# The key weights' path in four chunks, with a new order of every step, in a fused attention and FFN kernel

## The chip, the cores and the metric

The kernel runs on one core of a Trainium2 chip. The metric is the device time of one execution in microseconds (us); three executions before the change gave 151.39 us as their median (150.9 to 152.2).

The core has five instruction streams that run side by side and meet only at semaphores: TensorE (PE in the profile; its weight loads are listed as PEld), VectorE (DVE), ScalarE (ACT), GpSimd (POOL) and SyncE (SP), which here only issues DMAs. ScalarE can issue DMAs as well. Each stream executes in program order.

## The reference, cut to what matters

```python
xn = layernorm(x)                                     # x: 2048 x 448
q, k, v = heads(xn @ wqkv)                            # 16 heads of 28
pq, pk = q @ w_phi, k @ w_phi                         # 28 x 28 per head
phi(p) = concat(softmax(p), softmax(-p))              # 56 features per head
kv = phi(pk).T @ v;   z = sum over tokens of phi(pk)
o = (phi(pq) @ kv) / (phi(pq) . z + 1e-6)
h = xn @ w1 + b1
out = x + o @ wo + (h * tanh(softplus(h))) @ w2       # "mish", 1792 wide
```

## The kernel before, in words

**Tiles.** The 2048 tokens are 16 tiles of 128, handled as 8 pairs u = 0..7 (tiles 2u and 2u+1). The width 448 is three chunks of 128 rows and a tail of 64; the tail of two tiles shares one 128-row chunk, and so most matmuls work on half rows (64 of 128), two tiles side by side.

**Folded weights.** The feature map is folded into the weights: Wpk = Wk x blockdiag(w_phi) and Wpq = Wq x blockdiag(w_phi). For that Wk is loaded (`load_main`, line 272, three chunks, and `load_tail`, line 279, the last 64 rows twice), turned on TensorE (`w_tr`, line 550), brought to SBUF as WT, and multiplied with the block-diagonal Wbd (`w_mm`, line 573) into PSUM, from where the result goes to the tile Wpk. WT lies in the buffer Eq0, and so the profile shows its evacuations as writes of Eq. Wq is turned on the way by four DMA transposes (`load_qT`, line 284) and multiplied likewise into Wpq. In the kernel before, `w_tr` and `w_mm` work on halves h = 0, 1 of two chunks each: the first half's two turned chunks lie in two PSUM banks and are evacuated by ScalarE and VectorE side by side ("both"), the second half's by one instruction of one engine.

**Stages.** For each pair: statistics of the layer norm (`ln_stats`, VectorE, or three instructions of ScalarE), the reciprocal root (`ln_rstd`, ScalarE or GpSimd), the normalised pair xn (`ln_pair`, VectorE or GpSimd), its transpose xnT (`xT`, line 518, by TensorE with an evacuation, or by a DMA on SP). Then, on TensorE, V, K and Q of the pair (`v_mm`, `k_mm`, `q_mm`, all through `pair_part`, whose matmuls have line 438), each in a part 1 of 8 matmuls and a part 2 of 6. ScalarE takes exp(+) and exp(-) of K (line 623) and of Q (line 684), 4 pairs' V go through ScalarE (line 514) and 4 through VectorE (line 516). K's exponentials are normalised (`k_norm`: sum and reciprocal on VectorE, product on GpSimd), and all pairs are gathered into one KV matrix (`kv_mm`, line 652), which `kvz` masks and turns by a DMA into KVZ. Q's exponentials lie in one of three slots (`Eq_of`: slot 0 in the tile Eq, slots 1 and 2 in rows of actT) and are turned by one DMA per tile (`q_turn`, line 692, into EqT); pair u uses slot u mod 3, so that the exponentials of a later pair wait until the transposes of the earlier pair in the same slot have landed.

The FFN's first layer (`ffn1`) is 28 blocks of 14 matmuls (line 438 again, 512 columns) with one Mish on ScalarE each (line 703). Then come attention's second product (`nd`, line 726, with seven VectorE instructions), the transpose of o (`oT`, line 761), and the output sums of the FFN and of wo in common PSUM banks (`pair_out`, line 866; the last tiles in `ffn2` and `wo`, lines 828 and 844), which VectorE adds to x (line 793), and SP stores.

**PSUM.** There are 8 banks; most blocks take a pair (`take2`, line 391), the least recently used, and hold it until the evacuation.

**What sets the order.** Nothing is scheduled at run time: the table `ORDER` (line 147) names some 310 steps, `run_order` calls them in turn, and each appends its instructions to its engines' streams. Semaphore waits are worked out from the order (`Program.resolve`). In a name, the digits are the pair, tile or block, and a last letter is the engine (s: SP, a: ScalarE, d: VectorE, p: GpSimd, m: DMA): `lkms` loads the main part of Wk from SP, `wtk0b` turns half 0 of Wk and evacuates it on both engines. z12 is 12 matmuls on constants at the start.

Of the kernel before, what the change touches and what calls it, by code (L numbers as in the profile page):

```python
# [160 lines left out]
"""


# [5 lines left out]
def _kernel(es, nc, A_x, A_wqkv, A_w_phi, A_wo, B_w1, B_b1, B_w2, out):  # L169
# [62 lines left out]
    def Eq_of(u):  # L232
        if u % 3 == 0:
# [2 lines left out]

    oT_home = [(Wkv, 0, ["Wk", "Wv"]), (Wkv, 14 * P, []), (WqT, 0, ["Wq"]), (Wp[1], 0, ["Wp1"])]
    home_rows = {"Wk": [("Wk", 0), ("Wt", 0), ("Wt", 1)], "Wv": [("Wv", 0)], "Wq": [("WqT", g) for g in range(G)] + [("WqTd",)],
                 "Wp1": [("Wp", 1, h, c) for h in range(2) for c in range(2)]}

    homes_taken = set()

# [10 lines left out]
    def bank16(b):  # L253
        return PS.bitcast(BF16)[:, 2 * b * TCW:2 * (b + 1) * TCW]
# [7 lines left out]
    def pb(b):  # L262
        return ("ps", b)
# [140 lines left out]
    def take1():  # L404
        b = min((b for b in range(8) if b - b % 2 not in held), key=lambda b: used[b])
        touch(b)
        return b
# [139 lines left out]
                ap_on(mask[:, 2 * r:2 * r + 1], [[0, G], [1, 2], [0, DH]]), ALU.mult),  # L547
               r=[("Wraw",), ("mask",), ("Wbd0",)], w=[("Wbd", r)], tag=f"Wbd{r}")

    def w_tr(h, eng):  # L550
        b = take2(False) if eng == "both" else take1()

        def oT(c):
            if eng == "both":
                return bank16(b + c)[0:GP, 0:G * P].rearrange("p (g n) -> p g n", g=G)
            return bank16(b)[0:GP, c * G * P:(c + 1) * G * P].rearrange("p (g n) -> p g n", g=G)

        def tr(e):
            for c in range(2):
                for g in range(G):  # L560
                    ins = e.transpose(oT(c)[:, g, :], Wk[:, 2 * h + c, g * GP:(g + 1) * GP], ident[:])  # L561
            return ins
        r = rows_of("Wk")[:1 + 2 * h] + [("ident",)]
        if eng == "both":
            pe(tr, r, [pb(b), pb(b + 1)], f"wtr1{h}")
            for c, (en, res) in enumerate((("ACT", "WT"), ("DVE", "WU"))):
                evac(en, lambda c=c: WT[h][:, c], lambda c=c: oT(c), [pb(b + c)], [(res, h)], f"wtre1{h}.{c}")
            return
        pe(tr, r, [pb(b)], f"wtr1{h}")
        evac(eng, lambda: WT[h].rearrange("p c g n -> p (c g n)"), lambda: bank16(b)[0:GP, 0:2 * G * P], [pb(b)],  # L570
             [("WT", h), ("WU", h)], f"wtre1{h}")

    def w_mm(which, h, eng):
        b = take2(False)
        n = GP

        def lhs(c, g):
            if which:
                return WT[h][:, c, g, :]
            return WqT[0:GP, g, (2 * h + c) * P:(2 * h + c + 1) * P]  # L580

        def mm(e):
            for c in range(2):
                for g in range(G):
                    ins = e.matmul(bank(b + c)[:, g * n:(g + 1) * n], lhs(c, g), Wbd[:, g, :, 0:n // 2],  # L585
                                   start=True, stop=True)
            return ins
        pe(mm, ([("WT", h), ("WU", h)] if which else [("WqT", g) for g in range(G)] + [("WqTd",)]) + [("Wbd", 0), ("Wbd", 1)], [pb(b), pb(b + 1)], f"wmm{which}{h}")
        if which and eng == "both":
            for c, en in enumerate(("ACT", "DVE")):  # L590
                evac(en, lambda c=c: Wp[1][:, 2 * h + c, :], lambda c=c: bank(b + c)[:, 0:D], [pb(b + c)],
                     [("Wp", 1, h, c)], f"wmme1{h}.{c}")
            return
        if which:
            evac(eng, lambda: Wp[1][:, 2 * h:2 * h + 2, :], lambda: two(b, D), [pb(b), pb(b + 1)], [("Wp", 1, h, 0), ("Wp", 1, h, 1)],
                 f"wmme1{h}")
            return

        for c in range(2):
            evac(eng, lambda c=c: Wp[0][:, 2 * h + c, :].rearrange("p (g r n) -> p r g n", r=2, n=QP),  # L600
                 lambda c=c: bank(b + c)[:, 0:D].rearrange("p (r g n) -> p r g n", r=2, n=QP), [pb(b + c)],
                 [("Wp", 0, 2 * h + c)], f"wmme0{h}.{c}")

# [314 lines left out]
    for t in range(NT):  # L918
# [92 lines left out]
```

## Time and profile before

| what | value |
|---|---|
| median of the three runs | 151.39 us (150.9 to 152.2) |
| the profiled execution | 151.12 us |
| its span, first to last instruction | 149.2 us (1.92 us lie around it) |
| granted TensorE clock | 1.0 |
| busy: DVE, ACT, POOL | 101.7, 73.5, 41.7 us |
| DMA traffic | 17.24 MB, mean 116 GB/s; 271 to 303 GB/s in the slices from 3.7 to 14.9 us |

The profile is one execution. Its first part gives the busy time of each engine; the chain is followed back from the last instruction to what released it; the waits name the instruction that a waiting engine waited for; the timeline lists instructions by start, and an x behind a row merges neighbours of one form. Matmul ends are modelled and overlap the next start by up to 0.17 us, so starts are the better measure of TensorE's pace. For DMAs the landing is counted from the start of the issue.

### The profile page before, as it was taken

Reading aid. Unit: us, or ns where it says so; the run is one execution under the profiler, and the core shown is the slowest. Engines: PE = TensorE matmul, PEld = TensorE weight load, DVE = VectorE, ACT = ScalarE, POOL = GpSimd, SP = SyncE. Lnnn points to the kernel's source line nnn. Section 1 sums busy time; section 2 is a strip of 40 time slices with the busy share of each in tenths; the row PEclk is TensorE's granted clock in tenths of the full one; section 3 lists DMA queues with packets and bytes.
Section 4 is the critical chain, followed back from the end, with each engine's and each line's share of the span. In section 5 each row is a group of like instructions: output and inputs, shape, how many; then the busy total and the mean of one; then the engine's idle time right before and its main releaser. Section 6 shows DMA issues by size and latency. Waiting matters only on the chain.

```text
span 149.2 us, 3996 instructions
## 1 busy us (share of the span) xinstructions
PE 143.6 (96%) x1731; PEld 74.0 (50%) x1731; DVE 101.7 (68%) x226; ACT 73.5 (49%) x91; POOL 41.7 (28%) x60
## 2 busy tenths in 40 slices
PE   7799999999969999999999999999999999999993
PEld 2375555555424494444444455555555555455442
DVE  0999999999999303196675919999979495303342
ACT  3799999999679599766567580202000000000000
POOL 7607476999989930000000000000000000000000
DMA  5998988999939507999703030214100400700333
GB/s 132 282 303 271 202 136 117 177 241 203 178 72 196 88 4 146 245 320 195 157 4 62 4 62 0 42 24 40 28 4 0 123 4 19 166 4 0 125 121 123
DMA packets 39997, 17.24 MB, mean 116 GB/s; under 512 B 33964, under 2 KB 39212, under 8 KB 39980
## 3 DMA queue, kind: packets, MB, share of 16 engines
q1 hardware_dynamic: 39228, 16.64, 51.1%
q10 hardware_dynamic: 752, 0.35, 1.2%
q8 instruction: 13, 0.21, 0.6%
q14 instruction: 4, 0.03, 0.1%
HBM read 7.02 MB, written 1.84 MB: 59 GB/s over the span
## 4 chain that ended last, share of the span: by engine, by line
PE 86%; DMA 6%; ACT 3%; SPq 2%; DVE 1%; issue 0%; ACTq 0%
PE PS L438 44%; PE PS L866 31%; PE PS L828 3%; DMA Wkv<-in_A_wqkv_dram 3%; PE PS L726 2%; DMA EqT<-actT 2%; PE PS L652 2%; SPq L692 2%; PE PS L585 1%; ACT actT L684 1%; ACT actT L623 1%; PE PS L844 1%; PE PS L561 1%; ACT v_all L514 1%; SPq L270 1%; PE PS L509 1%
## 5 line engine op out<-in xcount | busy, mean ns | idle before, releaser
L438 PE MATMUL PS<-xnT,W 64*128 64x512 bf16 x392 | 45.1, 376 | 1.3 <-ACT actT L684 1.3
L703 ACT ACTIVATE actT<-PS,b1T 128x1024 bf16<-128x1024 f32 x28 | 29.8, 1112 | 20.9 <-PE PS L438 19.7
L866 PE MATMUL PS<-W,actT 64*128 64x448 bf16 x392 | 38.7, 349 | 0.0
L438 PEld LDWEIGHTS PS<-xnT,W 64*128 64x128 bf16 x392 | 18.1, 94 | 22.5 <-ACT actT L684 1.8
L866 PEld LDWEIGHTS PS<-W,actT 64*128 64x128 bf16 x392 | 18.4, 94 | 17.7
L635 POOL TENSOR_TENSOR actT<-actT,rSk 128x896 bf16<-128x896 bf16 x16 | 26.6, 1699 | 0.7 <-DVE rSk L633 0.7
L793 DVE TENSOR_TENSOR x_all<-PS,x_all 128x448 bf16<-128x448 f32 (+1 forms) x16 | 9.2, 615 | 16.1 <-PE PS L866 15.2
L631 DVE TENSOR_REDUCE Sk<-actT 128x32 f32<-128x896 bf16 x16 | 16.7, 1043 | 0.0
L741 DVE COPY Sq<-PS 128x16 f32<-128x16 f32 x32 | 4.0, 167 | 15.8 <-PE PS L726 15.8
L623 ACT ACTIVATE actT<-PS 128x896 bf16<-128x896 f32 x16 | 13.7, 923 | 0.9 <-PE PS L438 0.8
L438 PE MATMUL PS<-Wkv,xnT 64*128 64x448 bf16 x112 | 12.7, 349 | 0.0
L438 PE MATMUL PS<-Wpk,xnT 64*128 64x448 bf16 x112 | 12.6, 349 | 0.0
L438 PE MATMUL PS<-Wpq,xnT 64*128 64x448 bf16 x112 | 12.4, 349 | 0.0
L467 DVE BATCH_NORM_STATS2 stats<-x_all 128x6 f32<-128x448 bf16 x14 | 8.4, 604 | 3.7 <-DMA x_all<-in_A_x_dram 3.7
L749 DVE TENSOR_TENSOR v_all<-v_all 128x464 f32<-128x464 f32 x16 | 10.3, 642 | 0.6
L745 DVE TENSOR_TENSOR v_all<-PS,Sq 128x464 f32<-128x464 f32 x16 | 10.3, 641 | 0.5
L752 DVE TENSOR_TENSOR xn<-v_all,rden 128x448 bf16<-128x448 f32 x16 | 10.0, 625 | 0.6
L747 DVE TENSOR_TENSOR v_all<-PS,Sq 128x464 f32<-128x464 f32 x16 | 10.1, 630 | 0.0
L684 ACT ACTIVATE actT<-PS 128x896 bf16<-128x896 f32 x10 | 8.6, 920 | 2.2 <-DMA EqT<-actT 1.9
L438 PEld LDWEIGHTS PS<-Wpq,xnT 64*128 64x128 bf16 x112 | 5.5, 94 | 5.2
L438 PEld LDWEIGHTS PS<-Wkv,xnT 64*128 64x128 bf16 x112 | 5.4, 94 | 5.1
L438 PEld LDWEIGHTS PS<-Wpk,xnT 64*128 64x128 bf16 x112 | 5.4, 94 | 5.0
(89 smaller groups left out, 128.1 us busy)
## 6 DMA issues: line engine op xcount, KB each, us to landing
W<-in_B_w_dram SPq DMA_DIRECT2D x1, 1568.0 KB, 9.0
out_dram<-x_all SPq DMA_DIRECT2D x7, 224.0 KB, 2.3
W<-in_B_w_dram SPq DMA_DIRECT2D x3, 448.0 KB, 4.9
x_all<-in_A_x_dram SPq DMA_DIRECT2D x2, 448.0 KB, 4.7
x_all<-in_A_x_dram SPq DMA_DIRECT2D x3, 224.0 KB, 3.2
Wkv<-in_A_wqkv_dram SPq DMA_DIRECT2D x2, 336.0 KB, 4.7
Wo<-in_A_wo_dram SPq DMA_DIRECT2D x2, 336.0 KB, 3.8
W<-in_B_w_dram SPq DMA_DIRECT2D x2, 224.0 KB, 3.6
```

Of the source, the lines that this page charges most:

```text
L438: ins = e.matmul(o, lhs(c, k), rhs(c, k), start=part == "1" and c == 0, stop=part == "2" and c == 2)
L623: op("ACT", lambda e, s=s: e.activation(E_of(u)[:, s, :, :], two(b, D), ACT.Exp, scale=1.0 if s == 0 else -1.0), r=[pb(b), pb(b + 1)], w=[ ...
L631: op("DVE", lambda e: e.tensor_reduce(Sk[u][:, s, :], Eh(), AX.X, ALU.add), r=[("E", u, s)], w=[("Sk", u, s)], tag=f"Sk{u}.{s}")
L635: op("POOL", lambda e: e.tensor_tensor(Eh(), Eh(), ap_on(rSk[u][:, s, 0:1], [[1, 2 * H], [0, DH]]), ALU.mult), r=[("E", u, s), ("rSk", u, ...
L684: op("ACT", lambda e, s=s: e.activation(Eq_of(u)[:, :, s, :].rearrange("p i (h n) -> p i h n", n=64)[:, :, :, 0:QP], two(b, D).rearrange(" ...
L703: op("ACT", lambda e: e.activation(actT[:, fc, q * 1024:(q + 1) * 1024], bank(b, 2), ACT.Mish, bias=b1T[:, fc:fc + 1]), r=[("b1T",), pb(b) ...
L745: op("DVE", lambda e: e.tensor_tensor(tv(t1[i]), num(0), sx(1), ALU.mult), r=[pb(b), pb(b + 1), ("Sq", i, 1)], w=[("t1", i)], tag=f"ta{t}")
L747: op("DVE", lambda e: e.tensor_tensor(tv(t2), num(1), sx(0), ALU.mult), r=[pb(b), pb(b + 1), ("Sq", i, 0)], w=[("t2",)], tag=f"tb{t}")
L749: op("DVE", lambda e: e.tensor_tensor(t1[i], t1[i], t2, ALU.add), r=[("t1", i), ("t2",)], w=[("t1", i)], tag=f"tc{t}")
L752: op("DVE", lambda e: e.tensor_tensor(o_sb[(t // 2) % 2][:, t % 2, :].rearrange("p (h d) -> p h d", d=DH), t1[i][:, :, 0:DH], ap_on(rden[i ...
L793: op("DVE", lambda e: e.tensor_tensor(x_all[:, t, 0:n], bank(b)[:, 0:n], x_all[:, t, 0:n], ALU.add), r=[pb(b), ("x", t)], w=[("out", t)], ...
L866: ins = e.matmul(bank(places[par][0])[:, 0:D], l, r, start=fresh[par], stop=places[par][2] and i >= len(todo) - 2)
```

## The change

- Wk's path works on one chunk c = 0..3 at a time: one PSUM bank, four transposes and one evacuation for each `w_tr`, four matmuls and one evacuation for each `w_mm`. Chunk 3 alone waits for the loads of the tail. Wq's `w_mm` is split in four likewise, and only its chunk 3 waits for the doubled tail columns.
- Evacuations of the K side: the turned chunks 2 and 1 by ScalarE, 0 and 3 by VectorE; all four of Wpk, and all four of Wpq, by ScalarE.
- Wk's main part is SP's second load. x of pair 1, the bias and the main part of Wv are issued by ScalarE, behind its table load.
- The statistics that two of the tiles (7 and 15) had on ScalarE are on VectorE. Pairs 2, 4 and 5 are normalised by GpSimd (before: 7 and 0). Pair 1's transpose is evacuated by VectorE alone.
- The table is a new one. Of VectorE's work in the first 20 us it makes: statistics of tiles 6 and 7, normalisation of pair 3, then tiles 3, 2, 5, 4, normalisation of pair 1, its transpose's evacuation, tiles 14, 15, 12, 9, 8, 10, normalisation of pair 7, tile 11, V of pair 1. The load of tiles 12 to 15 stands on SP behind Wq's four transposes, where it stood ahead of them. Wo and W2 are loaded before KVZ is made, where it was after.

The diff, without most of the table:

```diff
 ORDER = """
-pm pw lx3s pp1 pp2 pp0 pk lx1s lkms lkts st6d lpa table pi st7a st2d st3d rs3t xn3d lvms rs1a xn1d lbs z12 lx2s lx0a
...
+lpa pp2 lx3s pm z12 st6d pi lkms table st7d pw lx1a lkts lba lvma bd rs3t wtk2a xn3d lx2s lqT2 wtk0d st3d pv wtk1a wmk2a
+xt3a wtk3d lqT1 wmk0a wmk1a st2d wmk3a st5d v31d rs1p lqT0 st4d xn1d rs2p lqT3 b1 qd lx6s v32a k31 lx0s wmq1a lx4s pp1
...
-    def w_tr(h, eng):
-        b = take2(False) if eng == "both" else take1()
...
+    def w_tr(c, eng):
+        b = take1()
+        to = bank16(b)[0:GP, 0:G * P].rearrange("p (g n) -> p g n", g=G)
 
         def tr(e):
-            for c in range(2):
-                for g in range(G):
-                    ins = e.transpose(oT(c)[:, g, :], Wk[:, 2 * h + c, g * GP:(g + 1) * GP], ident[:])
+            for g in range(G):
+                ins = e.transpose(to[:, g, :], Wk[:, c, g * GP:(g + 1) * GP], ident[:])
             return ins
...
+        pe(tr, rows_of("Wk")[:1 if c < 3 else 3] + [("ident",)], [pb(b)], f"wtr{c}")
+        evac(eng, lambda: WT[c // 2][:, c % 2], lambda: to, [pb(b)], [("WT", c)], f"wtre{c}")
...
+    def w_mm(which, c, eng):
+        b = take1()
+
+        def lhs(g):
+            if which:
+                return WT[c // 2][:, c % 2, g, :]
+            return WqT[0:GP, g, c * P:(c + 1) * P]
+
+        def mm(e):
+            for g in range(G):
+                ins = e.matmul(bank(b)[:, g * GP:(g + 1) * GP], lhs(g), Wbd[:, g, :, 0:GP // 2], start=True, stop=True)
+            return ins
+        r = [("WT", c)] if which else [("WqT", g) for g in range(G)] + ([("WqTd",)] if c == 3 else [])
+        pe(mm, r + [("Wbd", 0), ("Wbd", 1)], [pb(b)], f"wmm{which}{c}")
+        if which:
+            evac(eng, lambda: Wp[1][:, c, :], lambda: bank(b)[:, 0:D], [pb(b)], [("Wp", 1, c)], f"wmme1{c}")
             return
```

What the new table moves, at three places.

The first is the start of SP's queue, the loads. Before:

```order
L270 DMA x_all<-in_A_x_dram 128x896 x2
L273 DMA Wkv<-in_A_wqkv_dram 128x3x448
L281 DMA Wkv<-in_A_wqkv_dram 64x896 x2
L273 DMA Wkv<-in_A_wqkv_dram 128x3x448
L302 DMA b_rows<-in_B_b_dram 14x128
L270 DMA x_all<-in_A_x_dram 128x896
L270 DMA x_all<-in_A_x_dram 128x1792
L285 DMA_TRANSPOSE WqT<-in_A_wqkv_dram 128x448 x4
```

The change (the first L273 is Wk in both; the second, before, is Wv; the load of 1792 columns holds tiles 12 to 15):

```order
L270 DMA x_all<-in_A_x_dram 128x896
L273 DMA Wkv<-in_A_wqkv_dram 128x3x448
L281 DMA Wkv<-in_A_wqkv_dram 64x896 x2
L270 DMA x_all<-in_A_x_dram 128x896
L285 DMA_TRANSPOSE WqT<-in_A_wqkv_dram 128x448 x4
L270 DMA x_all<-in_A_x_dram 128x1792
```

One x load and Wv have left the queue ahead of Wq's transposes, and the load of tiles 12 to 15 has moved behind them.

The second is TensorE's first real work. Before:

```order
L376 MATMUL PS<-const-bfloat16-1.0 128x512 x12
L561 MATMUL PS<-ident,Wkv 112x128 x8
L509 MATMUL PS<-ident,xn 128x128 x7
L561 MATMUL PS<-ident,Wkv 112x128 x8
L509 MATMUL PS<-ident,xn 128x128 x7
L697 MATMUL PS<-ident,b_rows 128x14
L585 MATMUL PS<-Wbd,Eq 128x112 x16
L438 MATMUL PS<-Wkv,xnT 128x448 x22
```

The change (L556 is the turning of Wk, L571 the product, L509 the transpose of a pair, L674 that of the bias):

```order
L376 MATMUL PS<-const-bfloat16-1.0 128x512 x12
L556 MATMUL PS<-ident,Wkv 112x128 x12
L571 MATMUL PS<-Wbd,Eq 128x112 x4
L509 MATMUL PS<-ident,xn 128x128 x7
L556 MATMUL PS<-ident,Wkv 112x128 x4
L571 MATMUL PS<-Wbd,Eq 128x112 x12
L438 MATMUL PS<-Wkv,xnT 128x448 x8
L674 MATMUL PS<-ident,b_rows 128x14
L438 MATMUL PS<-Wkv,xnT 128x448 x6
L438 MATMUL PS<-Wpk,xnT 128x448 x8
L571 MATMUL PS<-Wbd,WqT 128x112 x8
L509 MATMUL PS<-ident,xn 128x128 x7
```

The products of Wk come between the turnings; V of pair 3 starts with one pair's transpose behind it where it was two, and the other pair's stands between the products of Wq.

The third is the middle of SP's queue, where the turning of Q's exponentials (EqT) meets the last chunks of W1 (L277). Before, from the last two transposes of xn on:

```order
L521 DMA_TRANSPOSE xnT<-xn 128x7x128 x2
L277 DMA W<-in_B_w_dram 128x1792 x2
L692 DMA_TRANSPOSE EqT<-Eq 128x8x128 x2
L692 DMA_TRANSPOSE EqT<-actT 128x8x128 x3
L692 DMA_TRANSPOSE EqT<-Eq 128x8x128
```

The change:

```order
L521 DMA_TRANSPOSE xnT<-xn 128x7x128 x2
L669 DMA_TRANSPOSE EqT<-actT 128x8x128
L277 DMA W<-in_B_w_dram 128x1792
L669 DMA_TRANSPOSE EqT<-actT 128x8x128
L669 DMA_TRANSPOSE EqT<-Eq 128x8x128
L669 DMA_TRANSPOSE EqT<-actT 128x8x128
L669 DMA_TRANSPOSE EqT<-Eq 128x8x128
L669 DMA_TRANSPOSE EqT<-actT 128x8x128
L669 DMA_TRANSPOSE EqT<-Eq 128x8x128
L669 DMA_TRANSPOSE EqT<-actT 128x8x128 x2
L312 DMA Wo<-in_A_wo_dram 128x3x448 x2
L312 DMA Wo<-in_A_wo_dram 64x448 x2
```

One chunk of W1 stands there where two stood (the other is loaded earlier), and a transpose of slot 2 (tile 5) has moved ahead of it. The tiles are 7, 6, 9, 5, 4, 13 before, and 5, then 4, 6, 8, 7, 9, 12, 10, 11 in the change; behind Wo follow tile 13 and W2.

More of the change, by code (lines that the diff above doesn't have):

```diff
@@ new lines @@
+wmq0a xn2p l1ts xt1d st14d st15d wmq2a wmq3a k32 k11 st12d rs7p st9d q11 xt2m st8d k12 st10d xn7d q31 rs4p v11d pp0 q12
+xn4p st11d v12d q21 rs5p st13d q32 q22 xn5p k21 st0d l1m2s l1m0s rs6p xt7m v21d k22 st1d v22a ep e3 rs0p v71a pk xt4m
+k71 v72a kn3.1 xn6d k72 xt5m k41 xn0d kn3.0 e2 xt6m xt0m v41d e5 k42 l1m1s v42d e4 q41 v51d q42 e6 e8 v52a kn2.0 k61
+v61d k62 kn4.0 k01 k51 kn7.0 kn4.1 k02 v62d q51 k52 q52 kn0.0 e7 q61 e9 v01d q62 e12 kn1.1 kn6.1 e10 f0.11 e11 kn1.0
+v02d f0.12 kn0.1 f1.01 f0.21 f1.02 f1.21 kn7.1 f1.31 f1.22 los kn2.1 q71 f1.32 f1.51 kn5.0 f0.22 e13 f1.52 q01 q72 q02
@@ L161 @@
+wo7F sto2 G42 wo7H sto0 wo42 g15 stt14 sto3 sto4 stt15
 """
@@ L238, in _kernel @@
     home_rows = {"Wk": [("Wk", 0), ("Wt", 0), ("Wt", 1)], "Wv": [("Wv", 0)], "Wq": [("WqT", g) for g in range(G)] + [("WqTd",)],
-                 "Wp1": [("Wp", 1, h, c) for h in range(2) for c in range(2)]}
+                 "Wp1": [("Wp", 1, c) for c in range(4)]}
     homes_taken = set()
@@ L346, in p_pads @@
             op("POOL", lambda e, i=i: e.memset(Eq_of(i).rearrange("p i s (h n) -> p (i s h) n", n=64)[:, :, QP:64], 0.0),
-               w=[("Eqp", i)] + ([(n, h) for n in ("WT", "WU") for h in range(2)] if i == 0 else []), tag=f"pp{i}")
+               w=[("Eqp", i)] + ([("WT", c) for c in range(4)] if i == 0 else []), tag=f"pp{i}")
     def p_mask2():
@@ L558, in tr @@
         def tr(e):
-            for c in range(2):
-                for g in range(G):
-                    ins = e.transpose(oT(c)[:, g, :], Wk[:, 2 * h + c, g * GP:(g + 1) * GP], ident[:])
-            return ins
[L563 to L567, printed above, removed]
-            return
@@ L569, in w_tr @@
[L569 to L602, printed above, removed]
@@ L625, in then @@
                    r=[pb(b), pb(b + 1)], w=[("E", u, s)], tag=f"exk{u}.{s}")
-        pair_part(f"k{u}", part, tok_works(u, Wp[1]), [("xnT", u), ("xnU", u)] + [("Wp", 1, h, c) for h in range(2) for c in range(2)], then)
+        pair_part(f"k{u}", part, tok_works(u, Wp[1]), [("xnT", u), ("xnU", u)] + [("Wp", 1, c) for c in range(4)], then)
     def k_norm(u, s):
@@ L922, in _kernel @@
         add(f"stt{t}", store, t, t + 1)
-    for h in range(2):
-        for eng, c in (("ACT", "a"), ("DVE", "d"), ("both", "b")):
-            add(f"wtk{h}{c}", w_tr, h, eng)
+    for ch in range(4):
+        for eng, c in (("ACT", "a"), ("DVE", "d")):
+            add(f"wtk{ch}{c}", w_tr, ch, eng)
             for which, n in ((0, "q"), (1, "k")):
-                add(f"wm{n}{h}{c}", w_mm, which, h, eng)
+                add(f"wm{n}{ch}{c}", w_mm, which, ch, eng)
     for q in range(2):
```

23 lines of the change are left out of this document (7 added, 16 removed).

## The prediction

> **What bounds the kernel now.** I read the span and the clock first, then the busy times, TensorE's waits, and the chain that ended last.
>
> ```profile
> core 0: 149.2 us, clock 1.000
> PE 143.6 (96%) x1731; PEld 74.0 (50%) x1731; DVE 101.7 (68%) x226; ACT 73.5 (49%) x91; POOL 41.7 (28%) x60
> PE PS L438 <- ACT actT L684: 1.3, 1, 1.3
> PE PS L561 <- DMA Wkv<-in_A_wqkv_dram: 0.9, 1, 0.9
> ```
>
> TensorE is busy 143.6 of 149.2 us at full clock, and all its waiting behind the first matmul is two gaps: 0.9 for Wk, and 1.3 for an exponential of ScalarE. So it is the bound, and the change can win only in such gaps, at the ends, or in work. The chain says when they fall:
>
> ```profile
> 1.73 4.87 DMA Wkv<-in_A_wqkv_dram
> 6.74 0.63 PE PS L561 x8
> 7.36 0.39 PE PS L509 x7
> 8.70 0.93 PE PS L585 x16
> 14.05 18.66 PE PS L438 x196
> 36.02 2.08 SPq L692
> 38.13 3.56 DMA EqT<-actT
> 146.22 0.02 issue
> ```
>
> From 6.74 to 146.22 TensorE pauses once, before 43.54; that pause goes back over ScalarE to a transpose of Q's exponentials (tile 4), issued at 38.13, that landed at 41.69. The rest of the span is 2.98 us of last addition and store, which the change leaves as they are, and the constants ahead of 6.74. TensorE's work stays too: the two order listings hold 16 turnings and 32 products before and after, in smaller groups. With both gaps closed the span would be 149.2 - 0.95 - 1.28 = 147.0; more is not to be had.
>
> **The change part by part.** *The start.* The rows of the first microseconds:
>
> ```profile
> 0.81 0.87 SPq L270 DMA_DIRECT2D x_all<-in_A_x_dram  x2
> 2.20 1.20 SPq L281 DMA_DIRECT2D Wkv<-in_A_wqkv_dram  x2
> 5.50 5.10 SPq L285 DMA_TRANSPOSE WqT<-in_A_wqkv_dram  x4
> 0.85 4.94 PE L376 MATMUL PS<-const-bfloat16-1.0 128*128 128x512 bf16 x12 [0.85 <-PEq L996]
> 6.74 0.63 PE L561 MATMUL PS<-ident,Wkv 128*112 128x128 bf16 x8 [0.95 <-DMA Wkv<-in_A_wqkv_dram]
> 3.73 0.58 ACT L459 ACTIVATE junk<-x_all 128x448 bf16<-128x448 bf16 x1 [1.20 <-DMA x_all<-in_A_x_dram]
> x_all<-in_A_x_dram SPq DMA_DIRECT2D x2, 448.0 KB, 4.7
> x_all<-in_A_x_dram SPq DMA_DIRECT2D x3, 224.0 KB, 3.2
> x_all<-in_A_x_dram ACTq DMA_DIRECT2D x1, 224.0 KB, 4.6
> WqT<-in_A_wqkv_dram SPq DMA_TRANSPOSE x4, 4.1
> ```
>
> Wk is issued one x load (0.87 / 2 = 0.43) sooner, and 224 KB fewer stand ahead of it. The issue alone moves TensorE's start T from 6.74 to 6.3; were the transfer as quick as the 224 KB loads (3.2), Wk would be there before the constants end at 5.79. I take T = 6.0 (5.79 to 6.74): -0.74. The three loads moved to ScalarE are issued from 2.5 on, in the 1.2 us in which it waited for x, so their issue costs nothing.
>
> [...]
>
> *Wk's chain.* The prices of an evacuation of one chunk, ScalarE and VectorE, of a whole pair's xnT and V, and of a statistic:
>
> ```profile
> 7.40 0.60 ACT L514 ACTIVATE Eq<-PS 112x512 bf16<-112x512 bf16 x1 [0.71 <-PE PS L561]
> L516 DVE COPY Eq<-PS 112x512 bf16<-112x512 bf16 x1 | 0.4, 416 | 0.0
> L514 ACT ACTIVATE xnT<-PS 128x896 bf16<-128x896 bf16 x1 | 0.9, 911 | 0.0
> L516 DVE CAST v_all<-PS 128x896 bf16<-128x896 f32 x4 | 4.3, 1076 | 0.5 <-PE PS L438 0.5
> 15.64 0.59 DVE L467 BATCH_NORM_STATS2 stats<-x_all 128x6 f32<-128x448 bf16 x1
> 16.36 0.59 DVE L467 BATCH_NORM_STATS2 stats<-x_all 128x6 f32<-128x448 bf16 x1
> 18.55 0.86 DVE L501 TENSOR_SCALAR xn<-x_all,mv,rstd 128x448 bf16<-128x448 bf16 x3
> 12.80 0.23 DVE L289 COPY WqT<-WqT 128x256 bf16<-128x256 bf16 x1
> ```
>
> Four turnings or products are 0.23 us (half of 0.63 less the 0.17 by which modelled ends overlap; a quarter of 0.93), a pair's transpose 0.39. Three chunks keep TensorE to T + 0.69. The first is read out from T + 0.43 (0.23 + 0.17 and a hand-over) to T + 1.03, so its product starts at T + 1.08: a gap of 0.39 where before a whole pair's transpose covered it. Then product, transpose of pair 3, last turning and two products reach T + 2.39; the last product waits for VectorE's copy of chunk 3 (0.17 pipe + 0.42 + two hand-overs after T + 1.93), to T + 2.6: 0.21 more. ScalarE, in turn, takes chunks 2 and 1 and the first product, each about 0.1 before the end of the one ahead, then pair 3's xnT from T + 1.9, and ends at T + 2.81: V starts at T + 2.86. The work in it is 0.92 + 0.93 + 0.39 = 2.24, so 0.62 is waiting; before, 2.74 of work took the 2.82 from 6.74 to 9.56. Term: +0.54. It is +0.4 if the hand-overs are shorter, and +0.8 if x of pair 1 (ScalarE's queue, 4.6) comes at 7.2 and holds VectorE up ahead of the chunk 3 copy.
>
> *Wq.* SP issues Wq's transposes after 0.43 + 0.47 + 1.24 + 0.43 us of loads instead of after 4.7: from about 3.4 to 8.5, the last one at 7.2. It lands 4.1 later, 11.3; before, the copy of the doubled columns, which needs all four, began at 12.80, so 9.33 + 3.4 bounds it from the quick side: 10.6. TensorE asks after V and K of pair 3 (22 matmuls at 18.66 / 196 = 0.095, and the bias): T + 5.06 = 11.1. Term: +0.15 (0 to +0.7, with ScalarE's 4.6 for a landing).
>
> *VectorE from 13 to 20 us.* Tiles 12 to 15 are issued behind Wq, at 8.5 instead of 5.06, and land 4.7 later: 13.2. From there stand six statistics of 0.72 (starts of neighbours), 0.86 for pair 7, one more statistic, a shift and V of pair 1 (1.08): its banks are free at 20.3. TensorE wants them for V of pair 2 about 84 matmuls after the Wq products: T + 5.06 + 0.15 + 1.32 + 8.0 = 20.5. So nothing, but with 0.2 in hand only, and beyond that each us is a us. Term: +0.1 (0 to +0.4, if the load is held up by 0.6, as each transpose behind the W1 chunks below).
>
> *The pause at 42.* Why tile 4 was late:
>
> ```profile
> 26.41 2.65 SPq L521 DMA_TRANSPOSE xnT<-xn  x2
> 29.11 1.07 SPq L277 DMA_DIRECT2D W<-in_B_w_dram  x2
> 30.23 4.39 SPq L692 DMA_TRANSPOSE EqT<-Eq  x2
> 34.66 4.83 SPq L692 DMA_TRANSPOSE EqT<-actT  x3
> 41.76 1.73 ACT L684 ACTIVATE actT<-PS 128x896 bf16<-128x896 f32 x2 [1.87 <-DMA EqT<-actT]
> 43.54 4.71 PE L438 MATMUL PS<-xnT,W 64*128 64x512 bf16 x42 [1.28 <-ACT actT L684]
> ```
>
> Behind two W1 chunks (896 KB), five transposes took 9.22 us to issue, where the undisturbed ones take 1.25 each, 6.25 in all: 2.97 were lost. ScalarE was ready at 39.89 and waited 1.87, of which TensorE lost 1.28; 0.59 lay in its full banks. In the change Q of pair 6 comes last, and needs tiles 6 and 7. Tile 7 is the fourth behind one chunk, with tile 5 ahead: 29.1 + 1.25 + 0.54 + 3 x 1.25 = 34.6, plus half the loss, 1.5, plus a landing of 3.56: 39.7, against 39.89 + 0.59. The pause is gone, unless the loss isn't halved: 41.2 costs TensorE 0.7, and as late as tile 4 costs all. Term: -1.13 (-1.28 to 0).
>
> *All else* goes at nothing. Behind 43.54 TensorE runs without a pause in the old order, while the three engines that feed it and read it out are busy 68, 49 and 28% of the span; that cover stays, and ScalarE's exponentials are of the same kind and count. What it costs where the cover is gone, the second rival prices.
>
> Sum: -0.74 + 0.54 + 0.15 + 0.1 - 1.13 = -1.08. The span becomes 148.1, the profiled time 151.12 - 1.08 = 150.0. The median lies 0.27 above the profiled execution; on it, 151.39 - 1.08 = 150.3.
>
> **The rivals.** *First: the pause stays.* Tile 7 is as late as tile 4 was, because the transposes, not the W1 chunk, fill the DMA engines; for it speaks that tile 7 is the seventh to be turned, as tile 4 was. Without the -1.13: 151.4.
>
> *Second, slower: Wo and W2 come too early.* Q's last block (pair 0) reuses the slot of tiles 12 and 13, and 13 stands behind four Wo loads and right ahead of W2 (1568 KB).
>
> ```profile
> 59.64 2.32 SPq L312 DMA_DIRECT2D Wo<-in_A_wo_dram  x4
> 62.63 4.11 SPq L692 DMA_TRANSPOSE EqT<-Eq  x1
> 53.44 1.73 ACT L684 ACTIVATE actT<-PS 128x896 bf16<-128x896 f32 x2
> DMA to landing us min/median/max: 3.1/3.3/9.2
> ```
>
> Tile 13 is issued about 41.7 + 3 x 1.25 + 2.4 = 47.9; ScalarE wants the slot at about 54, so a landing (of line 692's transposes, last row) of up to 6.1 is free. At 9.2 ScalarE, with every Mish queued behind that exponential, is 3.1 late, and TensorE 2.5 (0.59 in its banks): 148.1 + 2.5 is 150.6, and 152.8 on the median. Against it: before, only a transpose behind W2 suffered, and 13 is ahead of it.
>
> *Third: the start does not move.* Wk took 4.87 with two x loads ahead of it; if the transfers that now run beside it on the other queue stretch it by the 0.43 that its issue gains, T stays 6.74 and the sum is -0.34: 151.05. For it speaks that even ScalarE's lone x load took 4.6; against it, that it starts over 1 us behind Wk. [...]
>
> *Fourth: all goes well.* T = 5.79, no wait for Wq or V, the chain at +0.4, the pause gone: -0.95 + 0.4 - 1.28 = -1.83: 149.6.
>
> **How the numbers follow.** The forecast has 0.38, the first rival 0.18, the second 0.13, the third 0.14, the fourth 0.17. A measurement of this kernel can tell about 1%, 1.5 us, from no change (its three runs lie 1.3 us apart). Faster by more than that (under 149.9) is the fourth, most of it, and the quick side of the forecast: 0.31. Slower (over 152.9) is about half of the second and the pause kept together with late loads: 0.15. The rest, 0.54, is within 1%. The range, 149.0 to 152.5, reaches from beyond the fourth to most of the second.
>
> **What would show it.** Right: TensorE's wait for Wk under 0.3, a first gap near 0.4 behind three turnings, V near 8.9, no wait of line 438 for an exponential at 40 to 45, the span near 148.1. Wrong: V later than 9.3, a wait of ScalarE for EqT over 0.6 us before its first Mish or near 54, or a wait of TensorE for VectorE's V near 20.

## The result, and the profile after

The changed kernel takes 150.57 us (median of 20 runs, 150.14 to 151.44), the kernel before 151.47 beside it (20 runs, 150.89 to 152.20): a ratio of 0.994, 95% interval 0.9921 to 0.9960. So it is 0.9 us faster, 0.6%, which is less than the 1% that the prediction called told from no change. In the ratios here, executions more than 1.5% above the fastest of their kernel are left out; medians are of all.

The page of the changed kernel, with the busy times:

```profile
span 148.3 us, 3988 instructions
PE 143.7 (97%) x1731; PEld 75.9 (51%) x1731; DVE 100.7 (68%) x225; ACT 72.0 (49%) x83; POOL 44.4 (30%) x65
```

Its span is 0.9 us shorter than the 149.2 of before, with the same 1731 matmuls and the same busy TensorE. The gain lies in TensorE's waits (the columns are the total, the count, and the longest):

```profile
PE PS L556 <- DMA Wkv<-in_A_wqkv_dram: 0.4, 1, 0.4
PE PS L438 <- DMA xnT<-xn: 0.4, 1, 0.4
PE PS L571 <- ACT Eq L514: 0.3, 1, 0.3
```

The wait of 1.3 for an exponential is gone, the wait for Wk is shorter by half, and there are two new ones. The chain that ended last tells where they stand:

```profile
1.26 4.54 DMA Wkv<-in_A_wqkv_dram
...
5.94 0.42 PE PS L556 x4
...
6.38 0.61 ACT Eq L514
...
7.12 0.36 PE PS L571 x4
...
8.28 0.44 DVE Eq L516
...
8.76 0.37 PE PS L571 x4
...
14.22 4.29 DMA xnT<-xn
...
18.64 26.44 PE PS L438 x271
```

Read from above: Wk is on its way from 1.26 to 5.81, and TensorE turns its first chunk at 5.94, 0.80 sooner than before. The first product waits for ScalarE's evacuation until 7.12, and the last one for VectorE's copy, from 8.28. Then a transpose of xn (pair 2) lands at 18.5, and TensorE has waited 0.40 for it. Behind 18.64 nothing holds it: no pause at 42. SP's and then ScalarE's timeline at that place:

```profile
30.82 0.58 SPq L277 DMA_DIRECT2D W<-in_B_w_dram  x1
31.45 1.24 SPq L669 DMA_TRANSPOSE EqT<-actT  x1
...
36.06 2.37 SPq L669 DMA_TRANSPOSE EqT<-Eq  x1
38.47 1.31 SPq L669 DMA_TRANSPOSE EqT<-actT  x1
```

```profile
40.60 1.76 ACT L661 ACTIVATE Eq<-PS 128x896 bf16<-128x896 f32 x2
```

Tiles 4, 6, 8, 7 and 9 are issued from 31.45 to 39.78, in 8.33 us where undisturbed ones take 6.25: 2.08 are lost behind one W1 chunk, where the prediction counts 2.97 behind two. The exponential that needs tile 7 (issued at 36.06) starts at 40.60 without a wait in its row.

### The profile page after: what moved, and what is told of

The parts are those of the page before. It is cut to its first block, busy times and chain, and to the rows that moved or that the text cites. A ratio compares the mean times of both kernels' runs of the same rounds, so it can differ in the third digit from the quotient of the medians.

```text
span 148.3 us, 3988 instructions
## 1 busy us (share of the span) xinstructions
PE 143.7 (97%) x1731; PEld 75.9 (51%) x1731; DVE 100.7 (68%) x225; ACT 72.0 (49%) x83; POOL 44.4 (30%) x65
## 4 chain that ended last, share of the span: by engine, by line
PE 89%; DMA 6%; DVE 2%; issue 0%; ACT 0%; SPq 0%
PE PS L438 47%; PE PS L843 31%; PE PS L805 3%; DMA Wkv<-in_A_wqkv_dram 3%; DMA xnT<-xn 3%; PE PS L703 2%; PE PS L629 2%; PE PS L571 1%; PE PS L821 1%; DVE stats L467 1%; PE PS L556 1%; PE PS L509 1%; DVE xnT L516 0%; ACT Eq L514 0%; DVE x_all L770 0%
## 5 line engine op out<-in xcount | busy, mean ns | idle before, releaser
L843 PE MATMUL PS<-W,actT 64*128 64x448 bf16 x392 | 39.3, 349 | 0.0
L438 PEld LDWEIGHTS PS<-xnT,W 64*128 64x128 bf16 x392 | 18.8, 94 | 20.8 <-ACT actT L680 0.5
L718 DVE COPY Sq<-PS 128x16 f32<-128x16 f32 x32 | 4.1, 169 | 18.6 <-PE PS L703 18.5
L438 PE MATMUL PS<-Wkv,xnT 64*128 64x448 bf16 x112 | 13.2, 349 | 0.0
L467 DVE BATCH_NORM_STATS2 stats<-x_all 128x6 f32<-128x448 bf16 x16 | 9.7, 608 | 4.1 <-DMA x_all<-in_A_x_dram 4.1
L438 PEld LDWEIGHTS PS<-Wpk,xnT 64*128 64x128 bf16 x112 | 6.0, 94 | 4.4
L438 PEld LDWEIGHTS PS<-Wkv,xnT 64*128 64x128 bf16 x112 | 6.0, 94 | 4.3
```

Of the source, the lines that this page charges most:

```text
L438: ins = e.matmul(o, lhs(c, k), rhs(c, k), start=part == "1" and c == 0, stop=part == "2" and c == 2)
L467: op("DVE", lambda e: e.bn_stats(stats[:, t, :], x_all[:, t, :]), r=[("x", t)], w=[("st", t)], tag=f"bn{t}")
L843: ins = e.matmul(bank(places[par][0])[:, 0:D], l, r, start=fresh[par], stop=places[par][2] and i >= len(todo) - 2)
```

## The experiments

The steps in the diffs are those of the table; a line holds a step with its neighbours. In each call the kernels ran on one chip beside the kernel before, whose median differs from call to call (151.84, 151.46, 151.29, 151.63); so kernels of different calls are compared by their ratios.

**The pause, taken away alone.** The kernel before, with the second W1 chunk early:

```diff
-st15a st14d l1m0s v32a rs2p
+st15a st14d l1m0s l1m2s v32a rs2p
...
-v42d l1m2s e7 k52
+v42d e7 k52
```

> The kernel before, with one edit: the second of the two W1 chunks that SP issues ahead of five transposes of Q's exponentials is issued some 17 us earlier, behind the first W1 chunk; all else as before. Theory (the gain is the pause at 42 us, and W1 bytes ahead of the transposes make it): TensorE's 1.28 us wait for ScalarE goes, the span falls from 149.2 to 148.0 to 148.3, the median from 151.47 to 150.2 to 150.6, as good as the whole change. Rival (the gain is the earlier start and the finer chunks, and the pause only moves): 151.2 to 151.6. Second rival (the transposes themselves fill the DMA engines, the chunk doesn't matter): the wait stays over 0.9 us.

Measured: 151.20 (150.14 to 152.41, 12 runs) beside 151.84; ratio 0.9984, interval 0.9950 to 1.0018. The pause is gone, but the time moved less than the pause is long. TensorE's timeline of this kernel, at the start, at V of pair 3, and at 42 us:

```profile
6.91 0.99 PE L561 MATMUL PS<-ident,Wkv 128*112 128x128 bf16 x8 [1.96 <-DMA Wkv<-in_A_wqkv_dram]
...
11.23 2.25 PE L438 MATMUL PS<-Wkv,xnT 64*128 64x448 bf16 x22
...
42.23 6.21 PE L438 MATMUL PS<-xnT,W 64*128 64x512 bf16 x56
```

The row at 42.23 has no wait in brackets where before had 1.28. But this execution lost its gain at the start: TensorE waited 1.96 for Wk, and then 8 turnings took 0.99 instead of 0.63, and V began at 11.23 instead of 9.56. The order there is that of before; what differs most is the clock, which reads 0.50 from 7.5 to 9.5 where before had 1.00, and this is taken up below. Four of the twelve executions had a mean clock of 0.988 or 0.989. The median of the other eight is 151.12, beside 151.69 for the 32 executions of the kernel before with a full clock: 0.57 us for the chunk alone. In this profile the five transposes of Q's exponentials took 7.59 us to issue behind one chunk (30.67 to 38.26).

**The pause, put back.** The changed kernel with the two chunks side by side again:

```diff
-st0d l1m2s l1m0s rs6p
+st0d l1m0s rs6p
...
-k42 l1m1s v42d e4
+k42 l1m1s l1m2s v42d e4
```

> The changed kernel, with the W1 chunk put back: two chunks stand ahead of the transposes of tiles 4, 6, 8, 7 again, and everything else is the change's. In the change tile 7 landed at 40.46 and ScalarE wanted it at 40.60. Theory: tile 7 lands about 1.5 us later, ScalarE waits 1.4, TensorE 0.6 to 1.0: median 151.2 to 151.6, most of the gain gone. Rival (the gain is made at the start): 150.4 to 150.8, as the change.

Measured: 151.44 (150.98 to 151.78, 12 runs) beside 151.84; ratio 0.9988, interval 0.9962 to 1.0014. The waits of TensorE and ScalarE:

```profile
PE PS L438 <- ACT Eq L661: 1.1, 1, 1.1
...
ACT Eq L661 <- DMA EqT<-Eq: 1.5, 1, 1.5
```

and SP's timeline, with the two chunks and with tile 7:

```profile
31.39 1.06 SPq L277 DMA_DIRECT2D W<-in_B_w_dram  x2
...
38.05 2.14 SPq L669 DMA_TRANSPOSE EqT<-Eq  x1
```

With one more chunk ahead, tile 7 is issued at 38.05 instead of 36.06, the five transposes take 9.09 us, and the pause is back with 1.1 us. So the theory holds: one chunk more or less there decides whether TensorE pauses, in the old order (1.28 and none) and in the new one (1.1 and none). Without that edit the rest of the change brings nothing that its interval could tell from zero.

**x of pair 1 ahead of Wk again.**

```diff
-pi lkms table st7d pw lx1a lkts lba lvma
+pi lx1s lkms table st7d pw lkts lba lvma
```

> The changed kernel, with x of pair 1 issued by SP ahead of Wk, as before the change; bias and Wv stay with ScalarE. Theory: TensorE's first real work starts at 6.4 to 6.75 instead of 5.94, V of pair 3 0.5 to 0.8 later, but the lead was lost again to the transposed pair 2, which lands at 18.5 whenever TensorE comes: its 0.40 us wait there shrinks to about nothing, and the median rises by 0.1 to 0.5 only, to 150.7 to 151.1. Rival (the earlier start is a gain of its full size): +0.8, 151.4.

Measured: 153.40 (151.29 to 154.39, 12 runs) beside 151.84; ratio 1.0080, interval 1.0035 to 1.0125 (the two medians stand at 1.010). Every theory missed the size. Two things add up. Wk landed far later than in the kernel before, though the same two loads of x stand ahead of it on SP; only Wv and the bias run on ScalarE's queue beside it, Wv from 2.02 on. The DMA issues of this run (the last number is the median from issue to landing):

```profile
Wkv<-in_A_wqkv_dram SPq DMA_DIRECT2D x1, 336.0 KB, 6.1
Wkv<-in_A_wqkv_dram ACTq DMA_DIRECT2D x1, 336.0 KB, 7.2
```

Wk took 6.1 where it had 4.87 before. That fits the third rival, in which the transfers on the other queue stretch Wk's; in the change, x of pair 1 stands ahead of Wv on ScalarE's queue, Wv is issued only at 2.50, and Wk took 4.54 in one profile and 5.35 in the other. It is not shown to be the cause: Wq's transposes also start sooner here, at 4.07 where the kernel before has 5.50, and no run tells the two apart.

The other is the clock. The stretches of 1 us of this run (busy time of TensorE, granted clock, DMA share, GB/s):

```profile
6.50:7.50 1.00, 0.00 (x0) 0.87 1.10 306
7.50:8.50 1.00, 0.54 (x5) 0.50 2.73 193
...
13.50:14.50 1.00, 1.00 (x9) 0.71 1.05 416
14.50:15.50 1.00, 1.00 (x15) 1.00 1.08 323
```

The constants end at 5.07, TensorE stands still until 7.96, and while it stands the granted clock falls to 0.50; it stays there until about 14. So the first six microseconds of its real work ran at a granted clock of 0.50; the first 12 turnings took 1.50, where the change has 0.85.

**The same, with the wait filled.** The run before this, with z20 in place of z12: 20 matmuls on constants, whose output nobody reads.

```diff
-lpa pp2 lx3s pm z12 st6d pi lkms table
+lpa pp2 lx3s pm z20 st6d pi lx1s lkms table
```

> This is the earlier run with x of pair 1 issued by SP ahead of Wk (Wk waited for until 7.96, and TensorE at a granted clock of 0.50 from about 6.9 to 13.5), with 20 matmuls on constants at the start instead of 12; these have nothing to do with the result, and fill the wait. Theory: the clock fell because TensorE stood still for 2.9 us; with the wait filled the granted clock is 1.00 throughout, the turnings take 0.06 each again, V of pair 3 starts at about 11.0 instead of 12.1, and the time is 150.9 to 151.6 (ratio 0.995 to 0.999) where the run with 12 had 1.008. Rival: the half clock follows from the late landing or the loads and not from TensorE's idleness; the clock is 0.50 again behind Wk and the ratio stays near 1.008. If the constants run at half pace until their end, near 9.2, TensorE's work starts only then, and the ratio is 1.002 to 1.006 with the clock at 1.00.

Measured: 152.78 (152.44 to 153.20, 6 runs) beside 151.46; ratio 1.0091, interval 1.0060 to 1.0121. The time did not fall as forecast, since Wk landed still later (6.6 after its issue, where it was 6.1); but the clock did what the theory said. TensorE's timeline, and a stretch of this run:

```profile
8.46 0.85 PE L556 MATMUL PS<-ident,Wkv 128*112 128x128 bf16 x12 [0.24 <-DMA Wkv<-in_A_wqkv_dram]
...
11.45 0.93 PE L438 MATMUL PS<-Wkv,xnT 64*128 64x448 bf16 x8
```

```profile
8.50:9.50 1.00, 0.81 (x12) 1.00 0.86 83
```

Wk's turnings (12 in 0.85, where the run with 12 constants took 1.50) and V at 2.99 behind the start instead of 4.18: with the wait filled the clock stays at 1.00. Each of the six executions has a mean of 1.00, where eleven of the twelve with 12 constants have 0.977 to 0.989. So in these two runs the half clock came with the standing still, and not with the late load. What remains is the late load: a start 2.5 us later than in the change, and a ratio of 1.0091 against 0.9940, 2.3 us.

**The loads alone, in the old order.** The kernel before with the new loads:

```diff
-pp2 pp0 pk lx1s lkms lkts st6d lpa table pi st7a
+pp2 pp0 pk lkms lkts st6d lpa table lx1a lba lvma pi st7a
...
-xn3d lvms rs1a xn1d lbs z12
+xn3d rs1a xn1d z12
```

> This is the kernel before with its loads alone changed as in the change: Wk second on SP, x of pair 1, the bias and Wv issued by ScalarE behind its table load; halves, table and everything else stay. Theory 1, the one that I hold: Wk lands at 5.8 and TensorE starts at 5.9 to 6.0, but x of pair 1 now lands near 5.9 instead of ahead of 4.5, and the old order has both its statistics (2 x 0.72) ahead of the normalisation of pair 3 on VectorE, and the transpose of pair 1 ahead of Wk's products on TensorE; pair 3's xn comes at about 8.2, V of pair 3 starts at 10.3 to 10.8 instead of 9.56, and the time is 0.7 to 1.2 us longer than before (ratio 1.005 to 1.008), more if the clock falls in the wait. Theory 2: the load is what counts, whatever the order; V of pair 3 starts at 8.8, and the time is 0.7 us shorter (ratio 0.995).

Measured: 151.79 (151.63 to 152.11, 12 runs) beside 151.46; ratio 1.0025, interval 1.0004 to 1.0046. Theory 1 is right in its mechanism, with V where it was expected and 0.9 us on the profiled span, but only 0.4 us on the median. TensorE's timeline:

```profile
6.08 0.62 PE L561 MATMUL PS<-ident,Wkv 128*112 128x128 bf16 x8
8.19 0.56 PE L509 MATMUL PS<-ident,xn 128*128 128x128 bf16 x7 [1.49 <-DVE xn L501]
...
10.57 2.25 PE L438 MATMUL PS<-Wkv,xnT 64*128 64x448 bf16 x22
```

TensorE starts 0.66 sooner and reaches V 1.01 later: VectorE waits 1.23 for x of tiles 2 and 3, which now lands at 5.76 (4.44 before), and pair 3's xn queues behind their statistics. So the new loads need the new order of VectorE's work; in the old one they cost time.

**Halves with the new loads.** Two runs: the changed kernel with Wk's path in halves (first half read out by both engines, second by one), once in the table's order, and once with pair 3's normalisation ahead of VectorE's part of the first half:

```diff
-bd rs3t wtk2a xn3d lx2s lqT2 wtk0d st3d pv wtk1a wmk2a
+bd rs3t htk0b xn3d lx2s lqT2 st3d pv
...
-xt3a wtk3d lqT1 wmk0a wmk1a st2d wmk3a st5d
+xt3a htk1d lqT1 hmk0b st2d hmk1a st5d
```

```diff
-bd rs3t htk0b xn3d lx2s
+bd rs3t xn3d htk0b lx2s
```

> The changed kernel, with the path of Wk in two halves again (turned in halves of two chunks, first half read out by ScalarE and VectorE side by side, second by VectorE; product of the first half read out by both, of the second by ScalarE); loads, Wq and the order of the rest are the change's. Theory (the chunks' chain costs 0.8 us of waits, which eats the earlier start): V of pair 3 starts at 8.5 to 8.7 instead of 9.06; but pair 2's transpose still lands at about 18.5, so its wait grows from 0.40 to 0.7 to 0.9 and the median stays at 150.4 to 150.7. Rival (the four chunks are a gain): V of pair 3 after 9.2, median over 150.9.

> This is the changed kernel with Wk's path in halves, as in the kernel before, and the normalisation of pair 3 put ahead of VectorE's evacuation of the first half (the earlier run with halves had it behind, and lost 1.2 us there). Theory 1: halves cost less waiting than chunks, since fewer evacuations stand between the turnings and V: V of pair 3 starts at 8.6 to 8.9 (9.06 with chunks), and the time is 0.2 to 0.4 us below the changed kernel's (ratio 0.991 to 0.993). Theory 2: the chunks are worth nothing either way, V at 9.0 to 9.2 and the ratio 0.994. Theory 3: the chunks are a gain of the change, V at 9.4 or later and the ratio 0.996 to 0.999.

Measured: the first 151.65 (151.27 to 153.36, 12 runs) beside 151.84, ratio 1.0015, interval 0.9978 to 1.0053, with V at 10.34; the second 151.17 (150.79 to 151.95, 12 runs) beside 151.46, ratio 0.9987, interval 0.9968 to 1.0006. The first was partly a flaw of its own: VectorE's part of the evacuation stood ahead of pair 3's normalisation, and TensorE waited 1.3 for that. The second has it mended, and TensorE's timeline reads:

```profile
5.92 1.06 PE L561 MATMUL PS<-ident,Wkv 128*112 128x128 bf16 x8
...
8.10 0.65 PE L561 MATMUL PS<-ident,Wkv 128*112 128x128 bf16 x8 [0.73 <-DMA Wkv<-in_A_wqkv_dram]
...
10.04 0.93 PE L438 MATMUL PS<-Wkv,xnT 64*128 64x448 bf16 x8
```

V begins at 10.04, not at 8.6 to 8.9: theory 3. With Wk there early, the second half must wait 0.73 for Wk's tail rows, since chunk 3 is in it, and TensorE stands with nothing else to do; four chunks leave only the last of them to the tail, behind three turnings, a product and a transpose. So with this order of loads the chunks are no cost beside halves: V comes at 9.06 with them. Halves with the tail rows loaded first were not tried. Not all of this run's span of 149.3 is the start's: TensorE is 0.61 behind the changed kernel when it comes to pair 2, and loses another 0.3 at 49.02, where it waits for a Mish of ScalarE.

**The new wait for pair 2.** Three edits of the changed kernel, one added to the other (the first run has the first alone, the second the first and second, the third all), and the changed kernel itself beside the last two:

```diff
-v12d q21 rs5p st13d q32 q22
+v12d q32 q21 rs5p st13d q22
...
-k31 lx0s wmq1a lx4s pp1
+k31 lx4s lx0s wmq1a pp1
...
-ep e3 rs0p v71a pk xt4m k71
+ep xt4m e3 rs0p v71a pk k71
```

> This is the changed kernel with one step moved: part 2 of pair 3's Q (6 matmuls) stands ahead of part 1 of pair 2's Q, so that TensorE has 0.57 us more work before it first needs pair 2's xnT. Theory: the changed kernel's wait of 0.40 for that transpose (18.24 to 18.64) is covered; TensorE has no wait for xnT<-xn, the profiled span falls from 148.3 to 147.9 to 148.0, and the time from 0.994 of the kernel before to about 0.991 (0.35 us less than the changed kernel). Rival: the wait is not for the transpose but moves on, since ScalarE or the banks are what is late there: another wait of 0.3 to 0.4 between 18 and 22 us, and the ratio stays at 0.994.

> This is the changed kernel itself, once more, beside the two that follow. Its ratio should lie in the interval that it had, 0.992 to 0.996.

> This is the kernel with part 2 of pair 3's Q moved ahead of pair 2's, and with one load moved as well: SP issues x of tiles 8 to 11 ahead of x of pair 0 instead of behind it. Theory: moving Q alone gave nothing since the same lateness came out again at 26.6 us as a wait of 0.9 for pair 4's xnT, and that goes back over GpSimd's and VectorE's work to the x of tiles 8 to 11, which landed 6.1 us after its issue, at 15.9, and had VectorE wait 0.7. Issued 0.6 us sooner it lands near 15.2, VectorE does not wait, and pair 4's xnT comes 0.5 to 0.7 sooner: the wait at 26.6 falls to 0.2 to 0.4, and the time is 0.2 to 0.4 us below the changed kernel's of the same call. Rival: what holds pair 4's transpose is SP's queue (the turning of a tile of Q's exponentials ahead of it, and a landing of 4.8), so that the wait at 26.6 stays at 0.8 and the time at the changed kernel's.

> This is the kernel with part 2 of pair 3's Q and the load of tiles 8 to 11 moved, and with pair 4's transpose on SP ahead of the turning of tile 3's exponentials instead of behind it. Theory: the transpose is issued as soon as GpSimd has pair 4's xn, at about 20.4, lands near 25, and TensorE has no wait at 26; nothing is held up by the later turning, since SP has a gap there until pair 5's xn. Both waits for xnT are gone, V, K and Q run without a gap from 9 us on, and the time is 0.4 to 0.6 us below the changed kernel's of the same call (ratio 0.990 to 0.991). Rival: TensorE, now 0.4 to 0.5 us earlier, meets the next late thing, the transpose of tile 7, which in the changed kernel landed only 0.14 us ahead of ScalarE's exponential at 40.6: a wait of L438 for an exponential of ScalarE appears again near 42, and the time stays within 0.2 us of the changed kernel's.

Measured: 150.71 (150.19 to 151.80, 12 runs) beside 151.46, ratio 0.9959, interval 0.9933 to 0.9985, for the first. In the later call, beside 151.29: the changed kernel 150.48 (150.16 to 153.52, 8 runs), ratio 0.9935, interval 0.9909 to 0.9961; the second 150.62 (150.05 to 152.55, 12 runs), ratio 0.9969, interval 0.9933 to 1.0005; the third 150.64 (150.13 to 152.72, 12 runs), ratio 0.9965, interval 0.9934 to 0.9997. None of the three beats the change. TensorE's timeline of the first, then of the second:

```profile
17.93 2.50 PE L438 MATMUL PS<-Wpq,xnT 64*128 64x448 bf16 x20
...
26.61 0.93 PE L438 MATMUL PS<-Wpk,xnT 64*128 64x448 bf16 x8 [0.88 <-DMA xnT<-xn]
```

```profile
26.98 0.93 PE L438 MATMUL PS<-Wpk,xnT 64*128 64x448 bf16 x8 [0.69 <-DMA xnT<-xn]
```

The wait at 18 is covered, and another comes at 26, for pair 4's xnT: the rival of the first run, at a later place than it named. TensorE's earlier arrival is the smaller part of it. The chains of the two runs have for that transpose:

```profile
21.66 4.81 DMA xnT<-xn
```

```profile
21.75 5.09 DMA xnT<-xn
```

In the changed kernel it was issued at 21.55, took 2.99, and was wanted at 25.83, so that 1.3 were in hand. Why it took longer here is not shown. In the third run both waits are gone as large ones, its span is 148.6, and the wait for an exponential near 42 that its rival expected is not there; the time is the rival's all the same. The changed kernel's own second profile, whose Wk landed late, shows what a sooner start is worth:

```profile
6.75 0.85 PE L556 MATMUL PS<-ident,Wkv 128*112 128x128 bf16 x12 [1.65 <-DMA Wkv<-in_A_wqkv_dram]
...
9.73 0.93 PE L438 MATMUL PS<-Wkv,xnT 64*128 64x448 bf16 x8
...
18.75 2.06 PE L438 MATMUL PS<-Wpq,xnT 64*128 64x448 bf16 x20
```

It starts 0.81 us later than the first profile, reaches V 0.67 later, meets no wait at 18.75, and its span is 148.4 beside 148.3. The profile's view of pair 2's transpose alone (durations of the issue in ns, its start, and the time to landing) says in this execution:

```profile
L521 SPq DMA_TRANSPOSE xnT<-xn x1: 1265/1265/1265, 14.9 to 14.9; - x1
...
DMA to landing us min/median/max: 3.7/3.7/3.7
```

It was issued at 14.86 and landed at 18.52; in the first profile it was issued at 14.22 and landed at 18.51. So by these two profiles a start sooner than about 6.7 is worth next to nothing, since pair 2's transpose sets the pace at 18.5. A later start costs: with halves V came at 10.04, 0.31 behind this profile, and TensorE was 0.50 behind it at pair 2.

What sets that landing was not tested, but the traces point at SP's queue. The last load ahead of the transpose (tail rows of W1, L281) landed at 17.72 and 17.69 in these two profiles, 0.8 sooner. Where that load landed by 16.93 (both runs with halves, and the last two of the three edits) the transpose landed 2.94 to 3.58 after its issue. In the run with x of pair 1 first, though, the transpose took 4.22 when it was issued at 17.05, next to that load's landing at 17.55. No run moved the load.

**Before, with the pause gone and its start filled.** The kernel before, the chunk early, and 14 constants instead of 12:

```diff
-rs1a xn1d lbs z12 lx2s lx0a
+rs1a xn1d lbs z14 lx2s lx0a
...
-st15a st14d l1m0s v32a rs2p
+st15a st14d l1m0s l1m2s v32a rs2p
...
-v42d l1m2s e7 k52
+v42d e7 k52
```

> This is the kernel before with two edits: one of the two W1 chunks ahead of the transposes at 30 us is loaded early (as in the first run of this study), and the constants at the start are 14 instead of 12, which only fill more of TensorE's wait for Wk. Theory: what the whole change gains is the pause at 42 us, and its new start, chunks and loads come out even; so these two edits alone bring the changed kernel's time: no wait of L438 for an exponential near 42, the granted clock 1.00 in nearly all executions (in 4 of 12 of the first run it was lower, after waits for Wk of 2 us), and a ratio of 0.993 to 0.997. Rival: the start is worth something of its own in the changed kernel, and these two edits give 0.997 to 0.999.

Measured: 151.39 (150.73 to 152.09, 12 runs) beside 151.63; ratio 0.9983, interval 0.9959 to 1.0008: the rival's figure. TensorE's timeline:

```profile
19.39 0.93 PE L438 MATMUL PS<-Wkv,xnT 64*128 64x448 bf16 x8 [0.53 <-ACT actT L623]
...
42.00 6.37 PE L438 MATMUL PS<-xnT,W 64*128 64x512 bf16 x56
```

The pause is gone and the clock 1.00, but Wk came at 7.0, and TensorE lost 0.53 at 19.39. The row names an exponential of ScalarE, which ended at 19.31. The transpose of pair 2, which the same matmul waits for, landed only at 19.25, where it had 17.28 before: the early chunk now stands ahead of it on SP and landed at 18.30. In the first run of the experiments it was alike (18.26 and 19.08). So the chunk's early place has a price in the old order, which may be why the chunk alone brings less than the pause; no run tried another place. The two halves of the change (the chunk alone 0.9983 and 0.9984, all but the chunk 0.9988) add up to 0.3% where the whole has 0.6%; with intervals of 0.25 to 0.34% each, whether they help each other is left open.

## Why the prediction came out right

It said 150.3 on the median and 148.1 for the span; measured were 150.57 and 148.3. By its terms, against the profiled execution of before:

**The start, -0.74:** -0.80 in the first profile (5.94). The reason given for it was off in one point: the three loads on ScalarE do not wait for its table load. ScalarE's timeline:

```profile
1.27 1.28 ACT L315 ACT_TABLE_LOAD   x1 [1.27 <-PEq L973]
1.30 0.48 ACTq L270 DMA_DIRECT2D x_all<-in_A_x_dram  x1
...
2.50 0.41 ACTq L273 DMA_DIRECT2D Wkv<-in_A_wqkv_dram  x1
```

They are issued beside it, from 1.30 on. So x of pair 1 starts 0.04 behind Wk, and not over 1 us, as the third rival has it. Of the changed kernel's two profiles one has 5.94 and the other 6.75. Over all nine profiles with these loads TensorE starts at 5.92 to 6.24 in eight and at 6.75 in one; the three with the loads of before have 6.74 to 7.00. So the order does move the start, in most executions.

**Wk's chain, +0.54:** +0.80 (V at 9.06, or 3.12 behind the start, where 2.86 was worked out). The first gap was 0.33 (0.39 worked out), and the last product waited for VectorE's copy, as the working had it. The size failed: the first product came 0.10 later behind the start than worked out, and the last turning 0.17 later, just behind the landing of Wk's tail rows (7.77), which the working leaves out. In the second profile the chain took 2.98.

**Wq, +0.15, and V of pair 2, +0.1:** both 0. The products of Wq started at 11.49, and V of pair 2 at 21.29, without a wait.

**Not in the sum:** the wait of 0.40 for pair 2's xnT. The prediction followed VectorE and the banks for this pair, and not its transpose on SP, which took 4.29 to land. GpSimd's normalisation ahead of it is not what made it late, as the second profile shows (issued 0.64 later, landed at the same time).

**The pause, -1.13:** -1.28. Tile 7 was issued at 36.06 (36.1 worked out) and the exponential started at 40.60 without a wait; the pause comes back with the chunk. It was closer than forecast: the landing took 4.38, not 3.56, so that tile 7 was there at 40.44, 0.16 ahead of its use, where the working had 39.7.

The terms as measured, -0.80 + 0.80 + 0.40 - 1.28, make -0.88, where the span fell by 0.9. The terms of the start summed to +0.05 and came out as +0.40; the pause brought 0.15 more than forecast; the difference, 0.20, is what the sum was off. The step that failed in kind is the adding itself: the start's gain was put in at its full length, and the second profile shows that pair 2's transpose cuts it off. That the number came out all the same is partly luck: the terms of the start nearly cancel, in the forecast as in the profiles, and what is left is the pause.

The first rival fell with the chunk that brings the pause back. The second did not happen: tile 13 was issued at 48.78 and ScalarE's exponential for that slot ran without a wait. The third is false for the first profile, with Wk's 4.54; in the second its start came true (6.75, with Wk taking 5.35), and the time that it gave, 151.05, did not, since that execution took 150.42. The neighbour with x of pair 1 first fits its stretching: Wk took 6.1 beside Wv, and 4.87 ahead of it in the kernel before, though the sooner start of Wq's transposes is not ruled out. The fourth came near in its parts (no wait for Wq or V, the pause gone) and failed in the chain.

## What to carry to other kernels

An earlier start is worth only what the next supply can follow (here 0.81 us at the start were 0.1 on the span): before adding up gains along one engine, follow each later input (load, statistics, normalisation, transpose) to the time at which it would be asked for sooner. Where several transposes share a queue with a bulk load, the place of that load can decide a pause 10 us later (here of 1.28 us), and its new place can hold up other transposes (here one that landed at 19.25 and 19.08, where it had 17.28); look at what stands behind it in both. And a load that is made early must find its consumers ready: with halves, or with VectorE's old order, an early Wk gave a later V (10.04 and 10.57, where the change has 9.06).

## What the runs showed of the hardware

**In two profiled executions the granted clock fell, during a wait or just behind it.** Behind waits for Wk of 0.95, 1.04, 1.21 and 1.65 us the granted clock was 1.00; with waits of 1.96 (the kernel before with the chunk early) and 2.90 (x of pair 1 first) it fell to 0.50. The stretches of the first of these two:

```profile
6.50:7.50 1.00, 0.59 (x7) 0.75 1.07 348
...
9.50:10.50 1.00, 1.00 (x13) 0.55 0.71 92
```

TensorE stood still from 4.95 to 6.91 there. Stretches of 1 us that begin at whole numbers have 1.00 from 6 to 7, 0.50 from 7 to 10, and 0.80 from 10 to 11. With x of pair 1 first it stood still from 5.07 to 7.96, and the clock reads 0.87 from 6.5 to 7.5, 0.50 from 7.5 to 13.5, and 0.71 from 13.5 to 14.5. An estimate, in which every stretch with a mean in between holds one step between 1.00 and 0.50: the clock fell at 7.0 and rose at 10.4 in the first, and fell at 7.24 and rose at 14.08 in the second, so that 0.50 lasted 3.4 and 6.84 us. What sets these lengths no run shows. Of the changed kernel's first 20 executions none had a mean clock under 0.995, of its next 8 one (0.977, 153.52 us); of the kernel before 3 of the 35 in the first call of the experiments, at a median of 153.06 where the others had 151.69.

**In the changed kernel ScalarE issued DMAs beside its table load**, as the rows above show: the issue at 1.30 lies inside the 1.28 us from 1.27 on.
